# Scores of two slots in one visit of TensorE, with the last 64 keys in spare PSUM columns

## The chip, the cores and the metric

The kernel runs on one NeuronCore of a Trainium2 chip. The metric is device time in microseconds (us) of one execution. TensorE (PE) does matrix products into PSUM, an accumulator memory of eight banks with 512 fp32 columns on each of 128 partitions. VectorE (DVE), ScalarE (ACT) and GpSimd (POOL) do elementwise work; POOL does not touch PSUM. SyncE (SP) issues the DMA transfers of the kernel's steady part. Each engine works through its own list of instructions in order, and engines wait for each other through semaphores.

## The reference, cut to what matters

Attention with a top-k mask over 8 batches, 8 heads, 576 queries and keys and head size 64, followed by a two-layer block with a quick GELU on the 4608 x 512 result:

```python
scores = scale * np.matmul(q, k.transpose(0, 1, 3, 2))          # 576 x 576 per head
kth = np.partition(scores, -32, axis=-1)[..., -32:-31]
scores = np.where(scores >= kth, scores, -1e9)
attn = exp(scores - max); attn = attn / (sum(attn) + 1e-9)
x = (attn @ v) rearranged to (4608, 512)
h = x @ w_in                                                      # 512 -> 2048
out = (h / (1 + np.exp(-1.702 * h))) @ w_out                      # 2048 -> 512
```

## The kernel before, in words

The attention is cut into 144 **slots**. A slot is 128 rows of queries of two heads (64 rows of four heads for a head's last 64 queries, the "ends"); 18 slots make a batch. Odd batches begin with their two ends slots (heads 0 to 3, then heads 4 to 7), even batches end with them. For each slot the kernel does, in this order:

- `scores(n)` on PE: 8 products of 64 x 64 weights with 288 keys. They contract over 64 rows, so PE's array is split into four quadrants that work side by side. All four banks of the one tile `s_ps` are written: bank (head, half), 288 columns of each.
- `copy_scores(n)` on ACT: both heads' 576 scores to SBUF (tile `sc`), two instructions. `pair_up(n)` on DVE: maximum and minimum of the first half (from PSUM) against the second (from `sc`); after it and the copy, `s_ps` is free for the next slot.
- `find(n, 8)` on DVE: the 32 largest of each row by MAX8 and MATCH_REPLACE8. Inside it stand `pair_up(n+1)` (after 8 of its 14 instructions) and the reciprocal of slot n-1's sums (`invert`, after the next).
- `bounds(n)` on POOL: the row's threshold and maximum (`cut`, `low`). `mask(n)` and `exps(n)` on ACT (together `exponentials`): mask and exponential with row sums `den`.
- `invert(n)`: POOL adds 1e-9 (`some`), DVE takes the reciprocal (`rden`). `normalize(n)` on POOL. `split(n)`: ACT copies the words apart (2304 16-bit values per row), SP writes them to DRAM (`rows`). `turn_by_dma(n)`: SP issues a transposing DMA to `pt`.
- `values_of_two` on PE: the products with v for two slots, into two banks `o` of the pool `ps_t`. It begins with the last 64 keys (four quadrants again, tile `v_e`), then come the 512 others with all 128 rows of the array (`v_l`). `x_of_two` on ACT copies the result to `xT`.

The two-layer block fills PE in between: `hidden` (x @ w_in, 64 matmul instructions into a `ps_t` bank called `ph`), `tanh(True)` (ACT: tanh to `th`, then a copy `h` that frees the bank), `gate` and `combine` (POOL), and `project_one` (56 matmul instructions into `po`). An fp32 product is two matmul instructions. The pool `ps_t` has two banks, used in turn: hidden, hidden, o, o in each pair.

From slot 21 on, slots go in **pairs** (`steady_pair(n)`, n odd); the order on each engine is as written in that function, without a scheduler:

- PE: project, hidden, hidden around `scores(n+2)` (one `hidden` on either side of it), project, `scores(n+3)`, values of slots n-3 and n-2.
- ACT: exponentials(n-1); every second pair the previous result leaves `po` (`leave_parts`, L770); `prepare_some` (L268, `halves`: the queries and keys of a coming batch, one pair of heads at a time); split(n-1); copy_scores(n+2); mask(n), exps(n); two `tanh(True)`; split(n); copy_scores(n+3); x_of_two.
- POOL: normalize(n-1), gate, bounds(n), combine, normalize(n), gate, bounds(n+1), combine.
- SP: rows of n-1, what is due (`write_all`, `begin(0)`), the transpose for n-1, rows of n, `turns`, `begin(1)`, the transpose for n.

The queries and keys of a coming batch are transposed by DMA too (L282, `qk_t`). For odd batches b > 1 the last two pairs of heads are transposed at slot 18b-3 (`TURN = -3`, in `begin(0)` of pair n = 18b-3), since their buffers are taken until then; the second ends slot 18b+1 is the first that needs them.

Of the kernel before, what the change touches and what calls it, by code (L numbers as in the profile page):

```python
# [11 lines left out]
F32 = mybir.dt.float32  # L12
# [7 lines left out]
P = 128  # L20
# [13 lines left out]
def kernel(  # L34
# [27 lines left out]
    nc = tc.nc  # L62

    B, H, S, D = q.shape
# [3 lines left out]
    NF = S // P  # L68
    FULL = NF * P
    TAIL = S - FULL  # L70
    HALF = S // 2
# [7 lines left out]
    FIRST = (TAIL, 0)  # L79
# [9 lines left out]
    PAIRED = SETTLED + 1  # L89
    STEADY = PAIRED + 2  # L90
    WHOLE = 2
    RING = 7
    assert D == 64 and 2 * TAIL == P and C == NP * P and C == PIECE and B % 2 == 0
    assert TOPK == 32 and NP == 4 and NF == 4 and NG == 4 and CC == 4
# [2 lines left out]
    pool = lambda name, bufs, **kw: ctx.enter_context(tc.tile_pool(name=name, bufs=bufs, **kw))  # L97
    raws = const.tile([P, RING, 2 * PIECE], U32, name="raws")
    loads = pool("loads", 1)
    v_main = const.tile([P, NP, 2, NF, D], F32, name="v_l")  # L100
    qkt = pool("qkt", 6)
    scp = pool("scp", 4)
# [6 lines left out]
    diagonals = const.tile([P, 2, P], F32, name="by")  # L109
# [3 lines left out]
    score_banks = pool("ps_s", 1, space=PSUM).tile([P, 2, 2, 512], F32, name="s_ps")  # L113
    ps_t = pool("ps_t", 2, space=PSUM)
# [12 lines left out]
    def load_piece(n):  # L127
# [3 lines left out]
        else:  # L131
            src = moe_w_in[c * P : (c + 1) * P, g * PIECE : (g + 1) * PIECE]
        raw[n] = raws[:, n % RING, :]
        nc.sync.dma_start(raw[n], src.bitcast(U32))
# [29 lines left out]
    qT, kT, vv = {}, {}, {}  # L164
# [128 lines left out]
    def write_all():  # L293
        while writes:
            writes.pop(0)()
# [9 lines left out]
    slots = []  # L305
# [7 lines left out]
    st = [{} for _ in slots]  # L313

    def head_at(n, i):

        return 1 - i if n % 2 and slots[n][0] > 0 else i

    def scores(n):
        b, t, hps = slots[n]  # L320
        ps = score_banks
        quadrants = (0, 0), (1, 1), (0, 1), (1, 0)
        of = lambda p: slice(t * P + p * TAIL, t * P + (p + 1) * TAIL) if t < NF else slice(FULL, S)
        parts = [(i, p, slice(p * TAIL, (p + 1) * TAIL), of(p)) for i, p in quadrants]
        for c in range(2):
            for i, p, rows, cols in parts:
                on = slice(head_at(n, i) * D, (head_at(n, i) + 1) * D)
                nc.tensor.matmul(  # L328
                    ps[rows, i, c, 0:HALF],
                    lhsT=qT[b, hps[p]][on, cols],  # L330
                    rhs=kT[b, hps[p]][on, FIRST[i] + c * HALF : FIRST[i] + (c + 1) * HALF],
                )

    def copy_scores(n):
        ps = score_banks
        sc = st[n]["sc"] = scp.tile([P, 2, S], F32, name="sc")
        for i in range(2):
            to = sc[:, i, :].rearrange("p (c k) -> p c k", c=2)
            nc.scalar.copy(out=to, in_=ps[:, i, :, 0:HALF])  # L339
# [3 lines left out]
    def pair_up(n):  # L343

        b = st[n]["sc"][:, :, HALF:S]
        a = score_banks[:, :, 0, 0:HALF]
        ranked[n] = rank.tile([P, 2, 2, HALF], F32, name="ranked")
        for c, op in enumerate((ALU.max, ALU.min)):
            nc.vector.tensor_tensor(out=ranked[n][:, :, c, :], in0=a, in1=b, op=op)  # L349
# [47 lines left out]
    def exponentials(n, between=lambda: None):  # L397

        mask(n)
        between()  # L400
        exps(n)
# [220 lines left out]
    class Block:  # L622
        def __init__(self, place, rows):
            self.place, self.rows = place, rows
            self.whole = len(blocks_seen) < WHOLE
            blocks_seen.append(self)
# [91 lines left out]
    def weight_sums(to, x, y):  # L718

        def part(i, j):  # L720
            of = lambda name: half(name, i)[:, 2 * j : 2 * j + 2, :, :]
            nc.gpsimd.tensor_tensor(out=of(to), in0=of(x), in1=of(y), op=ALU.subtract)

        return [lambda i=i, j=j: part(i, j) for i in range(2) for j in range(2)]
# [7 lines left out]
    def project(put_off_leaving=False):  # L732
# [56 lines left out]
        if x.done == FC:  # L789
            leaving.append(leave if x.whole else leave_parts)  # L790
            if x is blocks_seen[WHOLE - 1]:
                summing.extend(weight_sums("t3", "b22", "b12"))
# [5 lines left out]
    def merge_some(count, engine=nc.gpsimd):  # L798
        for _ in range(min(count, len(merging))):
            merging.pop(0)(engine)  # L800
# [3 lines left out]
    def leave_all():  # L804
        while leaving:
            leaving.pop(0)()
# [17 lines left out]
    for n in by_slot:  # L824
        first = sum(map(len, list(by_slot.values())[:n]))
# [102 lines left out]
    def slot(n):  # L928
# [71 lines left out]
        if n == SETTLED:  # L1000
            copy_scores(n + 2)
# [16 lines left out]
    def dues(n):  # L1018

        preparing = prepare_by_dma, prepare_by_pe  # L1020
        todo = [later.pop(m, []) for m in (n, n + 1)]
        assert not any(fn in preparing for fn, _ in todo[1])

        def begin(i):
            for fn, args in todo[i]:
                if fn not in preparing:
                    fn(*args)

        some = [(fn, args) for fn, args in todo[0] if fn in preparing]

        def prepare_some():
            if some:
                fn, args = some.pop(0)
                fn(*args)

        return begin, prepare_some

    live = lambda m: 0 <= m < N
# [12 lines left out]
    def project_one():  # L1051
        if may_project(0):
            project(True)
# [95 lines left out]
    def steady_pair(n):  # L1149

        begin, prepare_some = dues(n)
        if live(n - 1):
            exponentials(n - 1)
        combine()
        merge_some(3)
        if n > STEADY + 8:
            project_one()
        hidden(ps_t)
        if n == STEADY + 8:
            tanh(True)  # L1160
            hidden(ps_t)
        leave_all()
        prepare_some()
        find(n, 8)
        if live(n + 2):
            scores(n + 2)
        hidden(ps_t)
        if live(n - 1):
            normalize(n - 1)
            split(n - 1)  # L1170
        write_all()
        gate()
        begin(0)
        if live(n - 1):
            turn_by_dma(n - 1)
        if live(n + 2):
            copy_scores(n + 2)
        if live(n):
            bounds(n)
        combine()  # L1180
        merge_some(3)
        if live(n):
            mask(n)
            exps(n)
        tanh(True)
        tanh(True)
        prepare_some()
        project_one()
        find(n + 1, 8)
        if live(n + 3):  # L1190
            scores(n + 3)
        held = [m for m in (n - 3, n - 2) if live(m)]
        o = [ps_t.tile([P, 512], F32, name="o", tag="tp")[:, 0:P] for _ in held]
        values_of_two(held, o)
        if live(n):
            normalize(n)
            split(n)
        write_all()
        while turns:
            turns.pop(0)()  # L1200
        begin(1)
        if live(n):
            turn_by_dma(n)
        gate()
        if live(n + 3):
            copy_scores(n + 3)
        x_of_two(held, o)
        if live(n + 1):
            bounds(n + 1)
# [54 lines left out]
```

## Time and profile before

| What | Value |
|---|---|
| median of 3 runs (lowest to highest) | 1384.13 us (1384.01 to 1385.76) |
| the profiled execution | 1387.0 us, of which the span of instructions 1385.2 us |
| busy share of the span | PE 97%, DVE 93%, ACT 84%, POOL 70% |
| mean granted PE clock | 0.987 |
| a steady pair (start of one `scores(n+3)` to the next) | 17.63 us in most pairs |

How to read it: times are microseconds from the start of the span. A row of the timeline has the start, the time from the first start to the last end of the instructions merged in it, engine, line, operation, output and input, shape, and count. Ends of matmuls are modelled and overlap the next group, so lengths on PE are taken from start to start. PEld is PE's weight load, which overlaps its matmuls. SPq rows are issues on SP.

### The profile page before, as it was taken

The page shows a single profiled execution, that of the slowest core. Times are in us where ns is not written, and L with a number is a line of the kernel's source. Part 1 is how long each engine was busy: PE and PEld are TensorE (multiplying, and loading weights), DVE is VectorE, ACT ScalarE, POOL GpSimd, SP SyncE. Part 2 cuts the span into 40 slices and gives each one's busy share as a digit, 9 for nine tenths or more (in the row PEclk, how much of TensorE's full clock was granted, in tenths as well). Part 3 has the DMA queues.
Part 4 walks back from the last instruction along what each step waited for, and adds up shares of the span by engine and source line. Part 5 has one row for each costly group of instructions (what it writes and reads, how often), then busy time and mean ns, then how long its engine had stood idle before and what let it go on. Part 6 is the DMA issues. An engine that isn't in the chain of part 4 may idle for free. (4 is left out here: it accounts for less than half of the span.)

```text
span 1385.2 us, 54404 instructions
## 1 busy us (share of the span) xinstructions
PE 1345.7 (97%) x22560; PEld 1209.1 (87%) x22560; DVE 1283.0 (93%) x3392; ACT 1165.2 (84%) x1930; POOL 963.8 (70%) x1758
## 2 busy tenths in 40 slices
PE   7889889999999999999999999999999999999998
PEld 5676568899998999999999999999999999999997
DVE  7999889999999999999999999999999999999912
ACT  6888778999998998999998998889998998888831
POOL 3777586677777777777776777777777777777770
PEclk9899999999999999999999999999999999999999
DMA  8552556988889776977798678887898878855640
GB/s 231 161 151 67 128 150 160 212 200 199 199 208 206 177 184 174 237 198 196 194 203 223 181 187 193 193 195 200 197 213 208 196 182 182 183 139 138 155 111 17
DMA packets 527223, 246.92 MB, mean 178 GB/s; under 512 B 458880, under 2 KB 505472, under 8 KB 526976
## 3 DMA queue, kind: packets, MB, share of 16 engines
q1 hardware_dynamic: 526544, 243.16, 71.7%
q8 instruction: 177, 2.90, 0.9%
q14 instruction: 70, 0.57, 0.1%
q10 hardware_dynamic: 432, 0.30, 0.1%
HBM read 46.01 MB, written 103.42 MB: 108 GB/s over the span
## 5 line engine op out<-in xcount | busy, mean ns | idle before, releaser
L375 DVE MAX8 top<-ranked 128x8 f32<-128x288 f32 (+1 forms) x1152 | 637.4, 595 | 0.0
L646 PEld LDWEIGHTS ph<-xT,win 128*64 128x64 f32 (+1 forms) x8736 | 479.7, 137 | 28.9 <-issue 25.0
L646 PE MATMUL ph<-xT,win 128*64 128x128 f32 (+1 forms) x8736 | 504.5, 273 | 0.0
L379 DVE MATCH_REPLACE8 ranked<-top,ranked 128x288 f32<-128x288 f32 (+1 forms) x864 | 462.3, 542 | 0.0
L479 ACT COPY sc<-pr 128x2304 uint16<-128x2304 uint16 x134 | 283.4, 2115 | 100.9 <-POOL pr L443 100.9
L443 POOL TENSOR_SCALAR pr<-pr,rden 128x576 f32<-128x576 f32 x268 | 198.0, 750 | 53.6 <-DVE rden L430 53.0
L417 ACT ACTIVATE pr<-sc,low 128x576 f32<-128x576 f32 x288 | 220.1, 771 | 0.0
L407 ACT ACTIVATE sc<-sc,cut 128x576 f32<-128x576 f32 x288 | 208.9, 781 | 5.6 <-POOL cut L393 5.6
L752 PE MATMUL po<-raws,h 128*64 128x128 f32 x2112 | 205.1, 273 | 0.2 <-POOL h L700 0.2
L752 PE MATMUL po<-wout,h 128*64 128x128 f32 x2112 | 205.2, 273 | 0.1
L349 DVE TENSOR_TENSOR ranked<-s_ps,sc 128x576 f32<-128x576 f32 x286 | 201.8, 747 | 0.3 <-ACT sc L339 0.3
L339 ACT COPY sc<-s_ps 128x576 f32<-128x576 f32 x286 | 168.5, 642 | 21.0 <-PE s_ps L328 13.6
L328 PE MATMUL s_ps<-qk_t 64*64 64x288 f32 x2304 | 177.5, 422 | 8.1 <-DVE ranked L349 7.7
L426 POOL TENSOR_SCALAR some<-den 128x2 f32<-128x2 f32 x132 | 29.3, 222 | 222.0 <-ACT pr L417 221.7
L675 POOL TENSOR_TENSOR th<-th,h 128x512 f32<-128x512 f32 x134 | 171.8, 1282 | 11.2
L752 PE MATMUL po<-wout,th 128*64 128x128 f32 x2176 | 165.2, 273 | 0.0
L752 PEld LDWEIGHTS po<-wout,h 128*64 128x64 f32 x2112 | 133.4, 137 | 0.6 <-POOL h L701 0.6
L752 PEld LDWEIGHTS po<-raws,h 128*64 128x64 f32 x2112 | 133.4, 137 | 0.5 <-POOL h L700 0.5
L328 PEld LDWEIGHTS s_ps<-qk_t 64*64 64x64 f32 x2304 | 76.1, 134 | 61.6 <-issue 14.4
L752 PEld LDWEIGHTS po<-wout,th 128*64 128x64 f32 x2176 | 127.7, 137 | 0.9 <-POOL low L394 0.4
L575 PE MATMUL o<-pt,v_l 128*64 128x128 f32 (+1 forms) x2240 | 124.8, 265 | 0.0
L575 PEld LDWEIGHTS o<-pt,v_l 128*64 128x64 f32 x2240 | 110.3, 137 | 10.1 <-issue 9.6
(111 smaller groups left out, 1631.3 us busy)
## 6 DMA issues: line engine op xcount, KB each, us to landing
rows<-sc SPq DMA_DIRECT2D x134, 576.0 KB, 3.8
qk_rows<-halves SPq DMA_DIRECT2D x24, 576.0 KB, 5.6
out_dram<-raws SPq DMA_DIRECT2D x68, 128.0 KB, 3.6
raws<-in_moe_w_in_dram SPq DMA_DIRECT2D x16, 512.0 KB, 4.9
raws<-in_moe_w_out_dram SPq DMA_DIRECT2D x16, 512.0 KB, 3.6
qk_l<-in_q_dram SPq DMA_DIRECT2D x28, 256.0 KB, 4.4
qk_l<-in_k_dram SPq DMA_DIRECT2D x28, 256.0 KB, 4.3
v_l<-in_v_dram SPq DMA_DIRECT2D x4, 1024.0 KB, 7.8
```

The lines of the kernel that those rows point to most:

```text
L328: nc.tensor.matmul(ps[rows, i, c, 0:HALF], lhsT=qT[b, hps[p]][on, cols], rhs=kT[b, hps[p]][on, FIRST[i] + c * HALF : FIRST[i] + (c + 1) * ...
L349: nc.vector.tensor_tensor(out=ranked[n][:, :, c, :], in0=a, in1=b, op=op)
L375: nc.vector.max(top[:, i, 8 * r : 8 * r + 8], of(r, i))
L379: nc.vector.match_replace(to, top[:, i, 8 * r : 8 * r + 8], of(r, i), LOWEST)
L407: nc.scalar.activation(sc[:, i, :], sc[:, i, :], AF.Prelu, bias=cut[:, i : i + 1], scale=SCALE, alpha=HUGE)
L417: nc.scalar.activation(pr[:, i * S : (i + 1) * S], sc[:, i, :], AF.Exp, bias=low[:, i : i + 1], accum_out=den[:, i : i + 1],)
L443: nc.gpsimd.tensor_scalar(pr[:, i, :], pr[:, i, :], st[n]["rden"][:, i : i + 1], 1.0, op0=ALU.mult, op1=ALU.mult)
L479: nc.scalar.copy(out=halves, in_=pr[:].bitcast(U16).rearrange("p (k h) -> p h k", h=2))
L575: nc.tensor.matmul(o[s][j * D : (j + 1) * D, cols], lhsT=lhsT, rhs=rhs, start=(s, j) not in halves[:k], stop=(s, j) not in halves[k + 1 :],)
L646: nc.tensor.matmul(ph[rows, i * P : (i + 1) * P], lhsT=win[:, c, f * P + rows.start : f * P + rows.stop], rhs=xs[:, x.place, c, :], start= ...
L675: nc.gpsimd.tensor_tensor(out=th[:], in0=th[:], in1=h, op=ALU.mult)
L752: nc.tensor.matmul(both_banks[y * TAIL : (y + 1) * TAIL, bank, to * P : (to + 1) * P], lhsT=a[:, i, :], rhs=weight(w, fs[i])[:, y, :], sta ...
```

## The change

`TOGETHER` is 24. From slot 24 on, scores are no longer taken slot by slot. In the second half of pair n, `scores_of_two` computes slots n+3 and n+4 one after the other, directly ahead of `values_of_two`. Of a head's 576 keys, 512 go to one whole bank of `s_ps` (slot parity and head choose the bank, so two slots fit in the four banks), and 64 go to columns 128 to 255 of the two `o` banks, whose first 128 columns the values use. Per slot the PE instructions are 8 of 512 and 8 of 64 columns, where they were 16 of 288.

`copy_asides` brings the 64-column parts to SBUF with four ACT copies per pair (64 partitions x 128 elements) into `by` (the tile `diagonals`). `copy_new` fills `sc` per slot: POOL copies the 64 keys of both heads out of `by`, ACT copies 1024 elements in one instruction. For slot n+4 that happens in the next pair, where `copy_scores` of that slot stood before; for slot n+3 at the end of this pair, between `gate` and `x_of_two`. `pair_up` reads the first 288 columns of the new banks. DVE's and SP's lists stay as they were. In the built program the first read of an `o` bank by `copy_asides` waits for the last matmul into that bank, which is one of the values'; the first write of the 64 columns into an `o` bank waits for the ACT copy `h` of the `ph` that had the bank.

```diff
+    TOGETHER = STEADY + 11
...
+    def scores_of_two(ms, aside):
+        for s, m in enumerate(ms):
+            b, t, hps = slots[m]
+            quadrants = (0, 0), (1, 1), (0, 1), (1, 0)
+            for first, count in ((0, FULL), (FULL, TAIL)):
+                for i, p in quadrants:
+                    rows = slice(p * TAIL, (p + 1) * TAIL)
+                    cols = slice(t * P + p * TAIL, t * P + (p + 1) * TAIL) if t < NF else slice(FULL, S)
+                    on = slice(head_at(m, i) * D, (head_at(m, i) + 1) * D)
+                    to = score_banks[rows, m % 2, i, :] if first == 0 else aside[head_at(m, i) ^ p][rows, P + s * TAIL : P + (s + 1) * TAIL]
+                    nc.tensor.matmul(
+                        to,
+                        lhsT=qT[b, hps[p]][on, cols],
+                        rhs=kT[b, hps[p]][on, FIRST[i] + first : FIRST[i] + first + count],
+                    )
+
+    kept = diagonals[:].rearrange("p a (c k) -> p (a c) k", c=2)
+
+    def copy_asides(aside):
+        blocks = slice(0, 4, 3), slice(1, 3)
+        for p in range(2):
+            rows = slice(p * TAIL, (p + 1) * TAIL)
+            for bank in range(2):
+                both = aside[bank][rows, P : 2 * P].rearrange("p (s k) -> p s k", s=2)
+                nc.scalar.copy(out=kept[rows, blocks[bank ^ p], :], in_=both)
+
+    def copy_new(m, s):
+        sc = st[m]["sc"] = scp.tile([P, 2, S], F32, name="sc")
+        nc.gpsimd.tensor_copy(out=sc[:, :, FULL:S], in_=kept[:, 2 * s : 2 * s + 2, :])
+        nc.scalar.copy(out=sc[:, :, 0:FULL], in_=score_banks[:, m % 2, :, :])
...
     def pair_up(n):
         b = st[n]["sc"][:, :, HALF:S]
-        a = score_banks[:, :, 0, 0:HALF]
+        a = score_banks[:, :, 0, 0:HALF] if n < TOGETHER else score_banks[:, n % 2, :, 0:HALF]
...
     def steady_pair(n):
         find(n, 8)
-        if live(n + 2):
+        if n + 2 < TOGETHER:
             scores(n + 2)
...
-        if live(n + 2):
+        if n + 2 < TOGETHER:
             copy_scores(n + 2)
+        elif live(n + 2):
+            copy_new(n + 2, 1)
...
         find(n + 1, 8)
-        if live(n + 3):
-            scores(n + 3)
         held = [m for m in (n - 3, n - 2) if live(m)]
-        o = [ps_t.tile([P, 512], F32, name="o", tag="tp")[:, 0:P] for _ in held]
+        banks = [ps_t.tile([P, 512], F32, name="o", tag="tp") for _ in held]
+        o = [bank[:, 0:P] for bank in banks]
+        ahead = [m for m in (n + 3, n + 4) if live(m)]
+        scores_of_two(ahead, banks)
         values_of_two(held, o)
...
         gate()
-        if live(n + 3):
-            copy_scores(n + 3)
+        if ahead:
+            copy_asides(banks)
+            copy_new(n + 3, 0)
         x_of_two(held, o)
```

## The prediction

> **What bounds the kernel now.** I read the page's first part, then the busy times of the steady stretch, then one pair on each engine, the chain from DVE and POOL into ACT, and last SP's queue. The page and the stretch first (columns: us, then busy us of PE, weight load, DVE, ACT, POOL, then clock):
>
> ```profile
> PE 1345.7 (97%) x22560; PEld 1209.1 (87%) x22560; DVE 1283.0 (93%) x3392; ACT 1165.2 (84%) x1930; POOL 963.8 (70%) x1758
> ...
> 701.36:718.99 17.63, 17.63 (x314) 16.14 (x313) 17.47 (x47) 15.15 (x25) 14.20 (x28) 1.00 0.85 186
> ```
>
> PE is never idle in this pair, at full clock, and DVE nearly so. Whether PE really streams is seen from start to start:
>
> ```profile
> 267.19 1.20 PE L328 MATMUL s_ps<-qk_t 64*64 64x288 f32 x16
> ...
> 701.36 1.20 PE L328 MATMUL s_ps<-qk_t 64*64 64x288 f32 x16
> 702.49 3.71 PE L646 MATMUL ph<-xT,win 128*64 128x128 f32 x64
> 706.04 0.61 PE L752 MATMUL po<-wout,th 128*64 128x128 f32 x8
> ...
> 709.19 1.20 PE L328 MATMUL s_ps<-qk_t 64*64 64x288 f32 x16
> 710.22 0.40 PE L575 MATMUL o<-pt,v_e 64*64 64x128 f32 x8
> 710.54 1.97 PE L575 MATMUL o<-pt,v_l 128*64 128x128 f32 x32
> 712.34 0.61 PE L752 MATMUL po<-wout,th 128*64 128x128 f32 x8
> ...
> 715.40 3.66 PE L646 MATMUL ph<-xT,win 128*64 128x128 f32 x64
> 718.99 1.20 PE L328 MATMUL s_ps<-qk_t 64*64 64x288 f32 x16
> ...
> 1292.37 1.20 PE L328 MATMUL s_ps<-qk_t 64*64 64x288 f32 x16
> ```
>
> The pair takes 718.99 - 701.36 = 17.63 us, and every group runs at its rate: a project (56 instructions, two at a time on two halves of the columns) 715.40 - 712.34 = 3.06, so 0.109 per 128 columns; 64 of hidden 3.55. From pair 23 to pair 139 it is (1292.37 - 267.19) / 58 = 17.68 per pair, 17.63 with few exceptions. So PE's list bounds the kernel, and anything else that stays under 17.63 is free.
>
> **PE's own work.** The first scores last 702.49 - 701.36 = 1.13, the second 710.22 - 709.19 = 1.03. The second has a four-quadrant group behind it, the first returns to 128 rows: 0.10 dearer. The project ahead of scores takes 709.19 - 706.04 = 3.15 where 3.06 is its rate: 0.09 for going in. hidden behind scores takes 3.55 against 32 x 0.109 = 3.49, some 0.05 more, and I give scores' first round the same 0.05. One visit to the quadrants so costs 0.10 + 0.05 in and 0.10 + 0.05 out: 0.30. The change removes one visit per pair: -0.30.
>
> Four instructions, one per quadrant, run as a round. A round of 288 columns is (1.03 - 0.05) / 4 = 0.245; with 0.109 for 128 that is 0.85 ns per column. So 512 columns are 0.435 (estimate), 64 columns 0.055 by that slope, or no cheaper than 0.109 if a weight load cannot hide under so short a round; the trace has no shorter one than 0.109. Per pair: before 8 x 0.245 = 1.96, after 4 x 0.435 + 4 x (0.055 to 0.109) = 1.96 to 2.18. PE's list alone would go to 17.63 - 0.30 + (0 to 0.22) = 17.33 to 17.55.
>
> Here a rule of the Trainium skill speaks against the change. The page TensorEngine Tiling (Array Packing), section Restrictions and Gotchas, says: "Different row tiles cannot access same PSUM bank simultaneously". The 64-column products of both row halves write to the same `o` bank. The trace does not agree: the row at 710.22 does that already for the values (both row halves of a slot into one bank), and its two rounds with the way out take 0.32 = 2 x 0.109 + 0.10. By the row the sharing costs nothing; by the rule the four 64-column rounds of a pair would take twice their time, 0.22 to 0.44 more.
>
> **ACT's chain, where I see the new bound.** The rows of ACT, DVE and POOL from one end of the values (712.34, call it T) on:
>
> ```profile
> 711.05 1.17 ACT L339 COPY sc<-s_ps 128x576 f32<-128x576 f32 x2
> 712.11 0.28 ACT L589 COPY xT<-o 128x128 f32<-128x128 f32 x1
> 712.57 0.27 ACT L589 COPY xT<-o 128x128 f32<-128x128 f32 x1 [0.18 <-PE o L575]
> 712.73 1.44 ACT L407 ACTIVATE sc<-sc,cut 128x576 f32<-128x576 f32 x2
> ...
> 715.50 0.19 ACT L417 ACTIVATION_READ_ACCUMULATOR pr<-sc,low 128x1 f32 x1
> 717.80 2.11 ACT L479 COPY sc<-pr 128x2304 uint16<-128x2304 uint16 x1 [2.12 <-POOL pr L443]
> 720.26 1.18 ACT L339 COPY sc<-s_ps 128x576 f32<-128x576 f32 x2 [0.34 <-PE s_ps L328]
> 721.33 1.45 ACT L407 ACTIVATE sc<-sc,cut 128x576 f32<-128x576 f32 x2
> ...
> 725.62 0.61 ACT L665 COPY h<-ph 128x512 f32<-128x512 f32 x1
> ...
> 730.78 0.45 ACT L589 COPY xT<-o 128x128 f32<-128x128 f32 x2
> ```
>
> ```profile
> POOL some L426 <- ACT pr L417: 221.7, 129, 3.4
> ...
> 715.77 0.22 POOL L426 TENSOR_SCALAR some<-den 128x2 f32<-128x2 f32 x1 [1.32 <-ACT pr L417]
> 716.03 0.17 DVE L430 RECIPROCAL rden<-some 128x2 f32<-128x2 f32 x1
> 716.29 1.47 POOL L443 TENSOR_SCALAR pr<-pr,rden 128x576 f32<-128x576 f32 x2 [0.30 <-DVE rden L430]
> ...
> 719.72 0.23 POOL L393 TENSOR_SCALAR cut<-top 128x4 f32<-128x4 f32 x1
> ```
>
> This is one chain: T, `xT` at T + 0.23, mask and exps of n-1 from T + 0.39 to 715.69, POOL's `some`, DVE's reciprocal (716.03 to 716.20), normalize, split at 717.80, copies, mask and exps of n, two tanh with their `h`, the last of which ends at 726.23 = T + 13.89. The wait list shows that its links really wait (129 times, 221.7 us, harmless so far). PE needs that `h` only where the values open the second `o` bank, at T + 17.63 - (712.34 - 710.22) = T + 15.51. Slack: 1.6.
>
> The change lengthens the chain and moves up its end. Copies first: one of 128 elements adds 0.45 - 0.28 = 0.17 when it follows another, one of 576 (712.11 - 711.05) / 2 = 0.53, so 1024 elements 0.53 + 448 x 0.8 ns = 0.89.
>
> - After T the second aside copy starts at T + 0.23, as `xT` did; three of the four come after T (0.51), then copy_new (0.89), then both `xT` (0.34). Mask starts at T + 1.97 instead of T + 0.39. Before, the copies of n+3 were done ahead of T.
> - From mask to split 717.80 - 712.73 = 5.07; a split 2.00 (from start to start of such a copy, below); copy_new 0.89; from mask to the end of the last `h` 726.23 - 721.33 = 4.90. Sum: 1.97 + 5.07 + 2.00 + 0.89 + 4.90 = T + 14.83.
> - PE's first 64-column round writes both `o` banks, so it waits for that `h`: about T + 14.93 with a tenth for the semaphore. PE's list reaches this place at 3.06 + 2 x 3.49 + 3.15 + 0.05 + 2 x 0.435 = T + 14.1. It now waits 0.8 us per pair.
> - From there: 0.11 to 0.22 for this slot's 64-column rounds, 0.87 and 0.11 to 0.22 for the next slot, 0.32 and 1.80 for the values: T' = T + 18.14 to 18.36. I take 18.25, the middle.
>
> Against 17.63 that is +0.62 in each of 59 pairs between two such visits (pairs 21 to 139): **+36.6 us**.
>
> What lies beside it: POOL's copy of 128 elements (between 0.23, the `cut` row, and 0.74, half of the normalize row; by columns 0.34) stands ahead of `cut`, which would come at T + 5.53 + (719.72 - 716.29) + 0.34 = T + 9.3, done by T + 9.53; mask(n) starts at T + 9.93. Cover 0.4, else its excess joins the chain. DVE needs 8.63 per find (731.31 - 722.68, below), 17.3 per pair, and gets a wait of some 1 us at the reciprocal; harmless under 18.25. The `xT` copies end at T + 2.1, hidden needs them at T + 3.06. `pair_up(n+2)`, for which both slots' products wait, ends at T + 1.97 + (716.03 - 712.73) + (722.68 + 1.42 - 716.03) = T + 13.34; two 512-column rounds later it is T + 14.3, 0.6 ahead of the `h`.
>
> **Where ACT has more in the chain.** In every second pair a result leaves and a copy for the next batch stands between exps and split:
>
> ```profile
> 722.68 1.42 DVE L349 TENSOR_TENSOR ranked<-s_ps,sc 128x576 f32<-128x576 f32 x2
> 731.31 1.42 DVE L349 TENSOR_TENSOR ranked<-s_ps,sc 128x576 f32<-128x576 f32 x2
> ...
> 733.96 0.98 ACT L770 ACTIVATE raws<-po 128x512 f32<-128x512 f32 x2
> 734.81 2.14 ACT L268 COPY halves<-qk_l 128x2304 uint16<-128x2304 uint16 x1
> 736.81 2.15 ACT L479 COPY sc<-pr 128x2304 uint16<-128x2304 uint16 x1
> ...
> L268 ACT COPY halves<-qk_l x24: 2112/2115/2146, 240.3 to 1123.1; 128x2304 uint16<-128x2304 uint16 x24
> ```
>
> 736.81 - 733.96 = 2.85, in a gap of 717.80 - 715.69 = 2.11: 0.74 too long. Leaves and copies both come every four slots, so the 23 copies after 248 us each have one: 23 x 0.74 = **+17.0**; 0 if they part company.
>
> **What is late next: three batches' keys.** Slot 18b+1 of odd b was scored in pair 18b-1 and now in pair 18b-3, the one that issues its transposes:
>
> ```profile
> 512.50 6.77 SPq L282 DMA_TRANSPOSE qk_t<-qk_rows  x2
> ...
> L282 SPq DMA_TRANSPOSE qk_t<-qk_rows x24: 2626/3846/5239, 256.7 to 1151.2; - x24
> ...
> DMA to landing us min/median/max: 6.3/6.9/8.3
> ...
> 514.67 1.20 PE L328 MATMUL s_ps<-qk_t 64*64 64x288 f32 x16
> ...
> 524.47 1.20 PE L328 MATMUL s_ps<-qk_t 64*64 64x288 f32 x16
> ```
>
> This is b = 3, whose pair has its T at 514.67 + (712.34 - 709.19) - 17.63 = 500.2. SP issues at T + 12.3, the second of the two 2.6 (the shortest issue) to 3.4 (half) later; I take T + 15.0, and it lands 6.9 after that: T + 21.9. Before, 524.47 was in time by 2.4. Now PE gets there at T + 15.1 and waits 6.8; with the shortest landing 6.2, with the longest 8.2. I take 6.5 for each of b = 3, 5 and 7: **+19.5**. SP's list is unchanged, so nothing moves these issues up; even batches transpose theirs a pair earlier.
>
> **Sum.** 1387.0 (the profiled execution) + 36.6 + 17.0 + 19.5 - 2.6 (the odd long pairs of before, 58 x 0.045, that the new wait swallows) = 1457.5. That execution is 2.9 above the median of 1384.1, so 1454.6 against the median, +5.1%. The bounds of the 64-column rounds move it by 6 each way, the 23 pairs down by 17, the keys by -1 to +5, the semaphore and copy estimates by 0.1 per pair, 6. The likeliest case's own range is 1425 to 1475.
>
> **Rivals.**
>
> - *ACT's chain fits* (it ends before T + 14.1: 0.8 us of my sum is wrong). For it: ACT is busy only 15.15 of 17.63, and 4 x 0.17 + 2 x 0.89 - 4 x 0.53 = 0.34 more work goes into it. Against: its idle time is those 2.1 us of waiting for POOL and DVE, in the chain. Then PE gains 59 x (0.08 to 0.30) = 5 to 18. With the keys' wait of 19.5 that is 1386 to 1399: chance 0.09.
> - *Faster*: PE remains the bound, as its busy row of 97% says, and stays so in the three batches. Place: the pair's first 64-column round; the point: nothing that PE waits for there or behind comes after T + 14.1. 1384 less 5 to 18: 1366 to 1379, chance 0.04. Against: the keys' landing alone.
> - *The keys cost nothing*, because the chain's own delay covers them: 1454.6 - 19.5 = 1435, chance 0.11. Against: 21.9 is well over 18.25.
> - *A second wait* in the chain: POOL's copy, `cut` and the merges of a leaving result delay mask(n) or `some(n)` by half a us or more per pair: +30 or more, 1485 to 1515. For it: cover of only 0.4. Chance 0.07.
> - *The banks take turns.* If row halves did so, each 64-column round would take twice its time: 59 x (0.22 to 0.44) = 13 to 26 more, about 1475. Against: the row at 710.22. Chance 0.03. The Trainium skill's page TensorEngine Tiling (Array Packing), section Restrictions and Gotchas, has this as a rule.
>
> **How the numbers follow.** My case has 0.66. Leaving out the second wait (0.07) above and the first two rivals (0.13) below, the range is 1415 to 1485. 0.2% of the time, 2.8 us, is about what a measurement of this kernel tells from no change. Faster comes from the second rival, same from the edge of the first: 0.04, 0.02, slower 0.94.
>
> **What would show it.** Steady pairs of some 18.2 us, 19 where both L770's and L268's successors stand; PE idle ahead of the 64-column rounds with ACT's `h` named; 0.5 us more of ACT between the values' end and mask for the asides; DVE waiting about 1 us at the reciprocal; PE waiting 6 us for `qk_t` near slots 55, 91 and 127. It would be wrong if PE's pairs stayed under 17.63, if mask started before T + 1.5, or if PE's wait named DVE or POOL.

## The result and the profile after

The changed kernel takes 1463.89 us (median of 6 runs, 1463.36 to 1465.74), the kernel before in the same session 1384.95 (1383.45 to 1389.93): ratio 1.0567, 95% interval 1.0549 to 1.0584. The profiled execution has a span of 1461.8 us against 1385.2. Line numbers below are those of the kernel that the row is from; in the changed kernel L346 is scores, L361 the aside copies, L367 the 1024-column copy, L442 the mask, L452 exps, L514 split, L610 values, L700 `h`, L787 project.

The page's busy line and its chain that ended last (PE had 47% of that chain before):

```profile
PE 1364.0 (93%) x22560; PEld 1214.5 (83%) x22560; DVE 1285.6 (88%) x3392; ACT 1193.3 (82%) x2050; POOL 990.5 (68%) x1878
...
ACT 26%; DVE 22%; PE 13%; issue 9%; POOL 8%; DMA 2%; SPq 1%; ACTq 0%; POOLq 0%; DVEq 0%
```

No engine is full any more. A plain pair, the next one with a leaving result and `halves` in it, and a stretch behind a late key transpose (columns as in the prediction):

```profile
705.61:723.97 18.36, 17.72 (x317) 16.25 (x315) 16.82 (x44) 14.95 (x26) 13.03 (x26) 1.00 0.88 211
...
723.97:742.98 19.01, 17.95 (x317) 16.13 (x314) 18.02 (x51) 17.81 (x29) 13.52 (x27) 1.00 0.71 195
...
528.00:541.00 13.00, 10.61 (x120) 8.18 (x122) 5.77 (x17) 5.31 (x10) 3.81 (x9) 0.74 0.54 134
```

Pairs alternate between 18.36 and 19.01. Taken from the start of one pair's values to the next, the pairs of slots 51, 87 and 123 take 23.61, 24.69 and 24.19, and the pairs behind them 20.42, 19.02 and 20.14; uneven pairs of the experiments below are taken in the same way, unless they are said to go from T to T. T is the end of the values, as in the prediction. ACT in the pair that starts at T = 705.61:

```profile
705.84 0.69 ACT L361 COPY by<-o 64x128 f32<-64x128 f32 x3 [0.62 <-PE o L610]
706.55 1.01 ACT L367 COPY sc<-s_ps 128x1024 f32<-128x1024 f32 x1
707.46 0.44 ACT L624 COPY xT<-o 128x128 f32<-128x128 f32 x2
707.78 1.46 ACT L442 ACTIVATE sc<-sc,cut 128x576 f32<-128x576 f32 x2
...
712.86 2.11 ACT L514 COPY sc<-pr 128x2304 uint16<-128x2304 uint16 x1 [2.11 <-POOL pr L478]
714.87 1.01 ACT L367 COPY sc<-s_ps 128x1024 f32<-128x1024 f32 x1
715.78 1.44 ACT L442 ACTIVATE sc<-sc,cut 128x576 f32<-128x576 f32 x2
...
720.07 0.59 ACT L700 COPY h<-ph 128x512 f32<-128x512 f32 x1
721.48 2.11 ACT L514 COPY sc<-pr 128x2304 uint16<-128x2304 uint16 x1 [0.82 <-POOL pr L478]
```

The mask starts at T + 2.17, the last `h` ends at 720.66 = T + 15.05. PE in the same pair:

```profile
705.61 0.61 PE L787 MATMUL po<-wout,th 128*64 128x128 f32 x8
...
719.25 1.09 PE L346 MATMUL s_ps<-qk_t 64*64 64x512 f32 x8 [0.37 <-ACT th L697]
720.13 0.31 PE L346 MATMUL o<-qk_t 64*64 64x64 f32 x4
720.71 0.27 PE L346 MATMUL o<-qk_t 64*64 64x64 f32 x2 [0.27 <-ACT h L700]
720.74 0.65 PE L346 MATMUL s_ps<-qk_t 64*64 64x512 f32 x2
...
721.65 0.31 PE L346 MATMUL o<-qk_t 64*64 64x64 f32 x6
721.77 0.28 PE L610 MATMUL o<-pt,v_e 64*64 64x128 f32 x2
...
723.97 0.61 PE L787 MATMUL po<-wout,th 128*64 128x128 f32 x8
```

PE waits twice. The first wait ends with `pair_up` of the other slot, whose last row on DVE ends at 719.15; the profile names `th`, which ends almost with it. The second time PE waits for the `h` that ends at 720.66. It goes on at T + 15.10, and the next pair starts 3.26 later. The list of waits (us in total, times, longest) has that `h` 120 times; before, a wait of values for `h` stood there with 1.5 us, 2 times:

```profile
POOL sc L366 <- ACT by L361: 131.6, 60, 9.2
...
DVE rden L465 <- POOL some L461: 80.3, 69, 3.7
...
PEld o L346 <- ACT h L700: 62.8, 120, 1.2
ACT by L361 <- PE o L610: 62.2, 88, 6.8
```

The late keys of batch 3, on SP and on PE:

```profile
523.48 5.90 SPq L283 DMA_TRANSPOSE qk_t<-qk_rows  x2
```

```profile
529.12 1.07 PE L346 MATMUL s_ps<-qk_t 64*64 64x512 f32 x2 [1.84 <-DMA qk_t<-qk_rows]
531.46 1.13 PE L346 MATMUL s_ps<-qk_t 64*64 64x512 f32 x3 [1.27 <-DMA qk_t<-qk_rows]
```

With PE's idle time at the keys comes a stretch of half clock: between 528 and 541 the granted clock is 0.74, which is 6.8 us at half speed in 13, and the same 0.74 stands in the 13 us from 869 and from 1214. So part of the six long pairs is clock, not waiting.

### The profile page after: what moved, and what is told of

Read it like the earlier page. It is cut to its first block, busy times and chain, and to the rows that moved or that the text cites. A ratio compares the mean times of both kernels' runs of the same rounds, so it can differ in the third digit from the quotient of the medians.

```text
span 1461.8 us, 54728 instructions
## 1 busy us (share of the span) xinstructions
PE 1364.0 (93%) x22560; PEld 1214.5 (83%) x22560; DVE 1285.6 (88%) x3392; ACT 1193.3 (82%) x2050; POOL 990.5 (68%) x1878
## 4 chain that ended last, share of the span: by engine, by line
ACT 26%; DVE 22%; PE 13%; issue 9%; POOL 8%; DMA 2%; SPq 1%; ACTq 0%; POOLq 0%; DVEq 0%
DVE top L410 11%; DVE ranked L414 8%; ACT pr L452 7%; PE o L610 6%; ACT sc L367 4%; ACT sc L514 3%; ACT sc L442 3%; ACT h L700 2%; PE po L787 2%; PE s_ps L346 2%; DVE ranked L384 2%; PE ph L681 2%; ACT halves L269 2%; POOL raws L809 2%; POOL pr L478 1%
## 5 line engine op out<-in xcount | busy, mean ns | idle before, releaser
L681 PE MATMUL ph<-xT,win 128*64 128x128 f32 (+1 forms) x8736 | 491.3, 273 | 0.0
L514 ACT COPY sc<-pr 128x2304 uint16<-128x2304 uint16 x134 | 283.7, 2117 | 120.9 <-POOL pr L478 120.9
L452 ACT ACTIVATE pr<-sc,low 128x576 f32<-128x576 f32 x288 | 220.3, 773 | 0.0
L442 ACT ACTIVATE sc<-sc,cut 128x576 f32<-128x576 f32 x288 | 209.4, 784 | 5.6 <-POOL cut L428 5.5
L787 PE MATMUL po<-raws,h 128*64 128x128 f32 x2112 | 205.1, 273 | 0.8 <-POOL h L735 0.8
L787 PE MATMUL po<-wout,h 128*64 128x128 f32 x2112 | 205.1, 273 | 0.1
L346 PE MATMUL s_ps<-qk_t 64*64 64x512 f32 x960 | 141.6, 617 | 34.8 <-ACT th L697 14.6
L787 PE MATMUL po<-wout,th 128*64 128x128 f32 x2176 | 165.2, 273 | 0.0
L346 PEld LDWEIGHTS o<-qk_t 64*64 64x64 f32 x960 | 56.3, 134 | 99.0 <-ACT h L700 62.8
L787 PEld LDWEIGHTS po<-raws,h 128*64 128x64 f32 x2112 | 133.4, 137 | 1.0 <-POOL h L735 1.0
L787 PEld LDWEIGHTS po<-wout,h 128*64 128x64 f32 x2112 | 133.3, 137 | 0.6 <-POOL h L736 0.6
L787 PEld LDWEIGHTS po<-wout,th 128*64 128x64 f32 x2176 | 127.9, 137 | 1.0 <-POOL th L710 0.6
L610 PE MATMUL o<-pt,v_l 128*64 128x128 f32 (+1 forms) x2240 | 128.2, 270 | 0.0
L366 POOL COPY sc<-by 128x128 f32<-128x128 f32 x120 | 34.9, 291 | 131.6 <-ACT by L361 131.6
L367 ACT COPY sc<-s_ps 128x1024 f32<-128x1024 f32 x120 | 121.9, 1016 | 1.5
L610 PEld LDWEIGHTS o<-pt,v_l 128*64 128x64 f32 x2240 | 113.6, 140 | 10.6 <-issue 9.6
```

Source lines behind the costliest of these rows:

```text
L346: nc.tensor.matmul(to, lhsT=qT[b, hps[p]][on, cols], rhs=kT[b, hps[p]][on, FIRST[i] + first : FIRST[i] + first + count],)
L367: nc.scalar.copy(out=sc[:, :, 0:FULL], in_=score_banks[:, m % 2, :, :])
L442: nc.scalar.activation(sc[:, i, :], sc[:, i, :], AF.Prelu, bias=cut[:, i : i + 1], scale=SCALE, alpha=HUGE)
L452: nc.scalar.activation(pr[:, i * S : (i + 1) * S], sc[:, i, :], AF.Exp, bias=low[:, i : i + 1], accum_out=den[:, i : i + 1],)
L514: nc.scalar.copy(out=halves, in_=pr[:].bitcast(U16).rearrange("p (k h) -> p h k", h=2))
L610: nc.tensor.matmul(o[s][j * D : (j + 1) * D, cols], lhsT=lhsT, rhs=rhs, start=(s, j) not in halves[:k], stop=(s, j) not in halves[k + 1 :],)
```

## The experiments

**Two rows of pairs that the theory explains one by one.** First the keys alone:

```diff
-        if b % 2 and hp > 1:
-            at(b * PER + TURN, turn)
+        if b % 2 and hp == 2:
+            at(b * PER + TURN - 1, turn)
         else:
             turns.append(turn)
```

> The changed kernel with the transposes of an odd batch's last two pairs of heads issued about half a pair sooner: in the second half of pair 18b-5, right behind the scores that free their buffers. Nothing else differs. Theory (three batches' keys come too late): the long pairs 51, 53, 87, 89, 123 and 125 (5.2, 2.1, 6.3, 0.7, 5.8 and 1.8 us over their neighbours, 21.9 in all) go, 1464 becomes 1442; the other pairs stay at 18.36 and 19.01. Rival (those long pairs come from the load on the DMA queues at a batch's start, whatever the order): 1464, or a stall that only moves to another pair, within 5 us of 1464.

Measured: 1444.92 us, ratio 1.0421 (1.0405 to 1.0436), 20 us less by the difference of the ratios. The six long pairs are gone (18.37 each), and with them the stretches of half clock. All other pairs stay at 18.37 and 19.02: the keys are a cost of their own.

Then the copy into `halves`, parted between POOL and ACT:

```diff
-        nc.scalar.copy(out=halves[:], in_=words.rearrange("p c (e h) -> p c h e", h=2))
+        parts = words.rearrange("p c (e h) -> p c h e", h=2)
+        nc.gpsimd.tensor_copy(out=halves[:, 0:4, :, :], in_=parts[:, 0:4, :, :])
+        nc.scalar.copy(out=halves[:, 4:, :, :], in_=parts[:, 4:, :, :])
```

> The changed kernel with the copy into halves (2.1 us, ScalarE, every second pair) parted: four of its nine blocks go to GpSimd, five stay, so that a leaving result (0.85) and the rest (1.2) fit the 2.1 us for which ScalarE waits for GpSimd. Theory: pairs of 19.01 become 18.36 to 18.5, 23 x 0.5 to 0.65 = 12 to 15 us less: 1449 to 1452. The rival (GpSimd, which makes the sums that ScalarE waits for, is late by as much as it takes over, 1.5 to 2 us) says 19.01 stays or grows: 1464 to 1485.

Measured: 1449.32, ratio 1.0453 (1.0436 to 1.0469). All pairs of 19.01 are at 18.37: this term, too, is what it was taken for.

The same two edits in the kernel before:

> The kernel before with two of the edits that made the changed kernel faster by 19 and 15 us: odd batches' last two key transposes a pair earlier, and the copy into halves parted between GpSimd and ScalarE. Theory (before is bound by TensorE's own list, keys are in time there, and the longer chain of a leaving result and halves still fits): no change, 1386 +- 4, ratio 0.998 to 1.002. The rival (these edits help any kernel, so they say nothing of the change) says 10 to 35 us less: 1351 to 1376.

Measured: 1384.92, ratio 1.0004 (0.9995 to 1.0013). Nothing. What these edits gain in the changed kernel, the change had put in.

**Is it the 0.4 us at the first 512-column round?** In the changed kernel both slots' scores are one tile, so PE's first round waits for the readers of the other slot as well. Two tiles in place of one:

```diff
-    score_banks = pool("ps_s", 1, space=PSUM).tile([P, 2, 2, 512], F32, name="s_ps")
+    ps_s = pool("ps_s", 1, space=PSUM)
+    score_banks = [ps_s.tile([P, 2, 512], F32, name=name) for name in ("s_ps", "s_pt")]
```

> The changed kernel with the score banks of odd and even slots as two PSUM tiles in place of one, so that the products of a slot wait only for the readers of its own bank; nothing else. The theory (the next pair's values are held by ScalarE's chain, which ends in the copy of h) says that the 0.5 us for which the first 512-column round waits for pair_up only moves to the 64-column round, which waits for h: pairs stay at 18.36 and 19.01, 1464 +- 4 us. The rival (the wait for pair_up, which comes from the two slots sharing a tile, is part of what sets the pair) says 0.3 to 0.5 us less per pair: 1434 to 1446.

Measured: 1464.82, ratio 1.0565 (1.0548 to 1.0581). PE in a plain pair:

```profile
721.21 1.09 PE L346 MATMUL s_ps<-qk_t 64*64 64x512 f32 x8
...
723.11 0.33 PE L346 MATMUL o<-qk_t 64*64 64x64 f32 x4 [0.64 <-ACT h L698]
```

The first wait has gone, and the second is longer by as much (0.64 = 0.37 + 0.27); pairs are 18.36 and 19.01 as before. So it is the wait for `h` that sets the pair.

**Lengthening the chain.** The 1024-column copy of slot n+3, done twice:

```diff
             copy_new(n + 3, 0)
+            nc.scalar.copy(out=st[n + 3]["sc"][:, :, 0:FULL], in_=score_banks[:, (n + 3) % 2, :, :])
```

> The changed kernel with the 1024-element copy of slot n+3 done twice in a row on ACT, 0.91 us more per pair; the second writes the same values again. Theory (chain): all of it shows, 59 x 0.91 = 54 us more, about 1518, pairs of 19.27 and 19.92. Rival (ACT has idle time to spare, PE or DMA set the pace): 1464 to 1470.

Measured: 1550.73, ratio 1.1185 (1.1159 to 1.1211), by the difference of the ratios 86 us more than the changed kernel. Where the clock is full, pairs are 19.41 and 20.07, 1.05 longer than in the changed kernel; the second copy starts 1.05 after the first. So each us of ACT in this place is a us of the pair: 59 x 1.05 = 62, where 54 were expected. In other stretches the pairs are 19.95 and 21.02, and there the granted clock drops again and again:

```profile
404.00:416.00 12.00, 10.09 (x146) 7.65 (x144) 12.00 (x36) 9.50 (x14) 8.14 (x16) 0.86 0.43 127
```

0.86 over 12 us is a stretch of 3.4 us at half speed; in these parts of the run such stretches come every 40.96 us. Ahead of this one PE had stood still twice:

```profile
409.11 1.09 PE L346 MATMUL s_ps<-qk_t 64*64 64x512 f32 x8 [1.25 <-DVE ranked L384]
...
411.19 0.37 PE L346 MATMUL o<-qk_t 64*64 64x64 f32 x2 [0.64 <-ACT h L700]
```

From T to T the pairs with such a stretch are 21.6, 1.5 us longer than 20.07, and there are 15 of them: the lost clock is the other part of the 86. But the same two waits do not always bring the clock down. From 640 to 836 they stand in every second pair, at full clock:

```profile
658.41 1.09 PE L346 MATMUL s_ps<-qk_t 64*64 64x512 f32 x8 [1.24 <-DVE ranked L384]
...
660.50 0.27 PE L346 MATMUL o<-qk_t 64*64 64x64 f32 x2 [0.64 <-ACT h L700]
...
640.00:836.00 196.00, 179.48 (x3116) 161.32 (x3110) 173.21 (x458) 172.67 (x283) 132.69 (x265) 1.00 0.76 181
```

**Was there slack in the kernel before?** The prediction gave its chain 1.6 us to spare. The two copies of slot n+3 there, done twice:

```diff
             copy_scores(n + 3)
+            for again in range(1):
+                for i in range(2):
+                    to = st[n + 3]["sc"][:, i, :].rearrange("p (c k) -> p c k", c=2)
+                    nc.scalar.copy(out=to, in_=score_banks[:, i, :, 0:HALF])
```

> The kernel before with the two copies of slot n+3 done twice on ACT, 1.06 us more per pair; the second pass writes the same values again. Theory (the same chain had 1.6 us to spare in the kernel before, mask starts only about 0.7 later): no change, pairs stay at 17.63, 1385 within 4 us. Rival (any work added to ACT at this place lengthens the pair): 60 x 0.7 to 1.06 = 42 to 64 us more, 1427 to 1449.

Measured: 1421.42, ratio 1.0250 (1.0234 to 1.0266). The theory falls in this point: pairs are 17.94 and 18.64 in turn, and the kernel is 35 us longer. ACT between one split(n) and the next, and PE's wait:

```profile
705.99 2.11 ACT L479 COPY sc<-pr 128x2304 uint16<-128x2304 uint16 x1 [0.65 <-POOL pr L443]
708.01 1.18 ACT L339 COPY sc<-s_ps 128x576 f32<-128x576 f32 x2
709.07 1.20 ACT L1210 COPY sc<-s_ps 128x576 f32<-128x576 f32 x2
...
710.45 1.49 ACT L407 ACTIVATE sc<-sc,cut 128x576 f32<-128x576 f32 x2
```

```profile
PEld o L575 <- ACT h L665: 37.6, 62, 0.8
```

There is a second loop, which does not go through PE at all: ACT's own list, with the waits for POOL and DVE that stand in it. Split ends, the copies and both `xT` follow without a gap, mask and exps, POOL and DVE make `pr`, split, and so on to the next split(n); in this run ACT waits for PE nowhere in it. Its length here is the pair, 17.94 and 18.64, so without the 1.06 us of repeated copies it would be 16.88 and 17.58, in the mean 17.23 against PE's 17.63. By this subtraction, an estimate, the kernel before had 0.4 us per pair to spare, not 1.6: the 1.6 were counted along the way from the values, and the other way round the loop was not looked at.

**Shortening the chain.** The 1024-column copy of slot n+3, done between the scores of n+3 and n+4, so that ACT does it while it waits for POOL ahead of split(n). The first two lines stand in `scores_of_two`, behind the products of a slot; in the old place only POOL's 128 columns are left:

```diff
+            if s == 0:
+                copy_main(m)
...
-            copy_new(n + 3, 0)
+            copy_last(n + 3, 0)
```

> The changed kernel with one ACT instruction moved: the 1024-element copy of slot n+3 stands behind the two tanh, ahead of split(n), where ACT idles 0.82 us, and no longer between the values' end and the next mask. Same work on every engine. Theory (the chain through ACT sets the pair): mask starts 0.91 sooner, the pair goes from 18.36 to about 17.45 and from 19.01 to 18.10, 59 x 0.91 = 54 us less, about 1410; if PE's own list (17.33 to 17.55) takes over, 1410 to 1416. Rival (PE's own groups have become dearer, by the short rounds or by sharing banks): 1464, as PE's work is the same.

Measured: 1510.40, ratio 1.0889 (1.0850 to 1.0927), slower instead of faster. The list of waits has a new line:

```profile
PE s_ps L346 <- ACT sc L368: 51.3, 57, 3.0
```

With one tile for both slots, the products of slot n+4 now wait for the copy of slot n+3: PE stands 0.9 us in the mean. The run decides nothing between the theory and the rival, since the edit put in a wait. The same edit with the two tiles of the run above:

> The same two tiles, and the 1024-element copy of slot n+3 issued between the products of slot n+3 and slot n+4, ahead of the split of slot n, so that it fills a wait of ScalarE for GpSimd and no longer stands between the values' end and the mask. Two loops are left: through TensorE, 18.36 less a copy of 0.9 = 17.45, and ScalarE's own list, 17.9 less one copy of 0.8 to 0.9 = 17.1 (0.7 more in pairs with a leaving result and halves). TensorE's own list is 17.33 to 17.55. So the theory says pairs of 17.45 to 17.6, with the extra work 18.1, the three late-key pairs as before: 1464 - 59 x 0.85 = 1414, 1405 to 1425. The rival (the pair is long because the 64-column rounds and the 512-column rounds cost TensorE more, and the wait for h is only where that shows) says that the pair stays at 18.2 to 18.4: about 1460. If the new place makes another wait, as in the run without the two tiles, the trace names ScalarE's copy ahead of the products of slot n+4.

Measured: 1447.95, ratio 1.0452 (1.0423 to 1.0482). Pairs are 17.98 and 18.33, where they were 18.36 and 19.01: the place was right, but the gain is 0.38 in the plain pairs and 0.68 in the others, not 0.9. The early copy also waits 14 times, 17.5 us in all, for its buffer, whose older contents are still being written out, and the pairs with such a wait take up to 21. What became of the other 0.5 us shows in the run with all four edits (two tiles, early copy, keys, parted `halves`):

> All of it: two score tiles, the early copy, the two key transposes of odd batches a pair earlier, and the parted copy into halves. By the theory every pair is at 17.45 to 17.6, which is TensorE's own list (17.33 to 17.55): against the kernel before (17.63 and 17.68 in the mean) 59 x 0.05 to 0.25 less, 1370 to 1383, so a little faster than the kernel before. If the parted copy fails, 23 x 0.6 more: 1384 to 1397. If the rival on TensorE's rounds were right, 1425 to 1440.

Measured: 1418.29, ratio 1.0224 (1.0205 to 1.0244), some 35 us above the expected range; pairs are 18.00 and 17.88. PE, ACT and POOL behind a T of 668.48:

```profile
668.48 0.61 PE L797 MATMUL po<-wout,th 128*64 128x128 f32 x8
...
668.70 0.70 ACT L365 COPY by<-o 64x128 f32<-64x128 f32 x3 [0.44 <-PE o L620]
669.42 0.43 ACT L634 COPY xT<-o 128x128 f32<-128x128 f32 x2
669.99 1.44 ACT L452 ACTIVATE sc<-sc,cut 128x576 f32<-128x576 f32 x2
...
669.46 0.29 POOL L374 COPY sc<-by 128x128 f32<-128x128 f32 x1 [1.55 <-ACT by L365]
669.73 0.23 POOL L438 TENSOR_SCALAR cut<-top 128x4 f32<-128x4 f32 x1
```

The mask starts at T + 1.51, right behind `cut` (669.73 + 0.23 = 669.96). POOL's 128-column copy waits 1.55 us for the aside copies, and `cut`, which needs nothing of them, stands behind it. So the two operations of `bounds` ahead of that copy:

```diff
+        if live(n + 1):
+            bounds(n + 1)
         if ahead:
             copy_asides(banks)
             copy_last(n + 3, 0)
         x_of_two(held, o)
-        if live(n + 1):
-            bounds(n + 1)
```

> The run with all four edits (1418), and the two small operations of GpSimd that make cut for the next mask issued ahead of its 128-column copy instead of behind it. In that run the mask starts 1.51 us after the end of the values, 0.14 after ScalarE's last copy, because cut stands behind a GpSimd copy that waits for the aside copies. Theory: mask 0.12 to 0.14 earlier, pairs 18.00 to 17.87, 59 x 0.13 = 8 us less: 1410, 1406 to 1414. The rival (what is left of the pair, 18.0 against TensorE's 17.5, is not on the way from the values to the mask) says 1418 unchanged.

Measured: 1395.76, ratio 1.0085 (1.0066 to 1.0104), 19 us less by the difference of the ratios, where 8 were expected. Pairs are 17.45 to 17.52, which is PE's own list. The rows, T = 664.91:

```profile
666.17 1.45 ACT L452 ACTIVATE sc<-sc,cut 128x576 f32<-128x576 f32 x2
...
671.24 2.11 ACT L524 COPY sc<-pr 128x2304 uint16<-128x2304 uint16 x1
```

```profile
664.33 0.23 POOL L438 TENSOR_SCALAR cut<-top 128x4 f32<-128x4 f32 x1
...
669.22 0.22 POOL L471 TENSOR_SCALAR some<-den 128x2 f32<-128x2 f32 x1 [0.15 <-ACT pr L462]
```

The mask is 0.25 earlier (T + 1.26), and from mask to split it takes 5.07 instead of 5.26 (in the plain pairs 5.14 instead of 5.38): `cut` and `low` had also stood, with their 0.5 us, in POOL's list between the aside copy and `some`, for which the chain waits. One edit of POOL's order counted at two places.

Then the mask itself ahead of the aside copies, in the 0.44 us for which ACT waits for the values (the next pair then begins with exps alone):

```diff
         if live(n + 1):
             bounds(n + 1)
+            mask(n + 1)
         if ahead:
             copy_asides(banks)
```

> The same, and the mask of the next slot issued ahead of the aside copies, in the 0.44 us for which ScalarE waits for the values. exps then follow the copies of xT directly: they start 2.25 us after the end of the values instead of 2.86, the last h ends 0.6 to 0.7 earlier than in the run with four edits, which is more than TensorE's wait of 0.5 there. Theory: TensorE's own list, 17.33 to 17.55 (17.49 by that run's own rows less its wait), is the pair again, and only the waits of the early copy for a score buffer are left over it (14 times, 16 us, of which half may be covered): 1418 - 59 x 0.5 = 1389, 1380 to 1398. The rival (the pair stays near 18.0 whatever ScalarE's order is) says 1410 to 1418.

Measured: 1435.68, ratio 1.0373 (1.0357 to 1.0388), 40 us worse than without. Pairs are 18.36 and 18.47. ACT and POOL, T = 471.89:

```profile
474.13 0.79 ACT L462 ACTIVATE pr<-sc,low 128x576 f32<-128x576 f32 x1
...
479.25 2.11 ACT L524 COPY sc<-pr 128x2304 uint16<-128x2304 uint16 x1 [3.49 <-POOL pr L488]
```

```profile
473.85 0.29 POOL L374 COPY sc<-by 128x128 f32<-128x128 f32 x1 [2.01 <-ACT by L365]
...
476.00 1.15 POOL L819 TENSOR_TENSOR raws<-raws 128x128 f32<-128x128 f32 x2
477.23 0.22 POOL L471 TENSOR_SCALAR some<-den 128x2 f32<-128x2 f32 x1
```

exps start at T + 2.24, as expected. But the aside copies come later, POOL's copy starts at T + 1.96 (T + 0.98 above), and behind it stand four operations of `combine` and the merges; `some` comes at T + 5.34 instead of the T + 4.31 above, though exps end at 475.8 (475.57 and 0.19 of the last read). The chain changed from ACT's list to POOL's.

**What is left, and a version that is faster.** With `cut` ahead the pairs are PE's, except eleven of 18.6 to 21.9, in which the early copy waits for a score buffer. A fifth one, paid with a tanh buffer and a place for `xT`:

```diff
-    scp = pool("scp", 4)
+    scp = pool("scp", 5)
-    PLACES = 4
+    PLACES = 3
-    thp = pool("thp", 8)
+    thp = pool("thp", 7)
```

> The run with cut ahead (1396, pairs of 17.45 to 17.51 and eleven longer ones of 18.6 to 21.9), with a fifth score buffer, for which one of eight tanh buffers and one of four places for xT are given up. In that run the early copy of slot n+3 waited 19 times, 22.5 us in all, for the write of an older slot's halves out of the same buffer. Theory: these waits go, the long pairs come down to 17.5 to 18, 20 to 25 us less: 1371 to 1376, faster than the kernel before by about 0.8%; pairs are TensorE's own list. The rival (fewer tanh buffers and places make a new wait, ScalarE for the project's reads of th and h) says 17.6 or more per pair, 1380 to 1396.

Measured: 1381.08, ratio 0.9964 (0.9951 to 0.9978): faster than the kernel before, by 0.36%, about half of what was expected. All six runs are below all eleven of the kernel before in the same session (at most 1382.66 against at least 1383.09). Two pairs of it:

```profile
677.00:712.00 35.00, 35.00 (x630) 32.19 (x628) 34.73 (x92) 31.93 (x55) 27.68 (x55) 1.00 0.91 201
```

PE is full again, and the steady pairs are 17.46 and 17.53 against 17.63. What keeps the gain below 59 x 0.13 = 8 us is six longer pairs (18.0 to 18.7). In five of them PE waits for a transposed `pt`, 0.2 to 0.8 us; in the sixth it waits 0.3 for `h`.

## Why the prediction was right, and where it was not

The forecast was 1454.6 in a range of 1415 to 1485; it came to 1463.9, slower by 5.7% where 5.1% was said. The mechanism was the one forecast: ACT's chain from the end of the values to the last `h`. Of the 9.3 us that it missed, the pairs make +6.4, `halves` -2.0 and the keys +2.4; 2.9 more were taken off because the profiled execution before lay above its median, which the one after does not. By its steps:

- **PE's own work.** Right. Its list alone was put at 17.33 to 17.55 per pair; where nothing else holds it, it takes 17.45 to 17.53. A 64-column round costs what the slope said: from 721.65, where the last two begin, to 721.77, where the first products of the values begin behind them, it is 0.12, so 0.06 apiece where 0.055 to 0.109 was said.
- **ACT's chain as the new bound.** Right, and shown from both sides: one us more in it is one us more per pair, and when it is made short enough PE's list returns. Behind the copies its terms were sized to 0.02: from mask to split 5.08, the split 2.01, the 1024-column copy 0.91, and from mask to the last `h` 4.88, against 5.07, 2.00, 0.89 and 4.90.
- **The copies after T.** This term was too small. The aside copies were priced at 0.17 apiece, after copies of 128 rows; these take 64 rows each and follow at 0.24 (three of them from 705.84 to 706.55). So mask started at T + 2.17 instead of T + 1.97, `h` ended at T + 15.05 instead of T + 14.83. PE went on 0.05 behind it, not 0.10, and the rest took 3.26, near the lower end of 3.21 to 3.43. So the pair is 18.36, at the upper end of 18.14 to 18.36, where 18.25 was taken. Over 59 pairs that is 43 us for 36.6, the largest part of the miss.
- **Pairs with a leaving result and `halves`.** 0.65 instead of 0.74: 15 for 17.0 us, and gone when a part of the copy moves to POOL.
- **The keys.** The landing was put too late. In the pair of slot 51, T is 511.86 and PE goes on with the second keys at 531.46 = T + 19.6, not T + 21.9. A plain pair is there at T + 15.1, so the keys add 4.5 us and not 6.5 (at slots 87 and 123 it is 5.6 and 5.1). But half clock comes with it, which no step had, and it costs more than was saved: the six pairs together are 21.9 us over 18.36 each, where 19.5 was forecast. The sum came near by two errors of opposite sign, which is luck.
- **Slack of 1.6 in the kernel before, and what ACT's idle time is.** Wrong. Repeating two copies there cost 35 us. The step followed the chain from the end of the values to `h` and compared it with PE; it left out the loop that closes through ACT's own list. For the changed kernel the omission did no harm, because there the way through PE is the longer one.
- **`pair_up` 0.6 ahead of `h`.** Right. It ended at 719.15, T + 13.54 instead of T + 13.34, and the two 512-column rounds behind it were done 0.53 ahead of `h` (720.13 against 720.66). PE waits 0.37 for it at the first round, and two tiles showed that this costs nothing.
- **DVE's wait at the reciprocal.** About 1 us was said; in the pair shown it is 1.33 (711.09), and the list of waits has 80.3 us in all against 26.7.
- **The rivals.** *ACT's chain fits* and *faster* are refuted for this kernel; they come true only with the edits of the last runs. *The keys cost nothing* is refuted too: with the keys earlier the kernel is 20 us shorter. *A second wait in POOL's list* did not occur in the changed kernel (mask(n) starts 0.6 behind `cut`), but three of the experiments ran into it. *The banks take turns*: the Trainium skill's page TensorEngine Tiling (Array Packing), section Restrictions and Gotchas, has it as a rule; the 0.06 us above, with two row halves writing into one bank, and PE's list of 17.45 speak against it. The rule would add 0.22 to 0.44 to that list. By the measurement, which decides, row halves write one bank side by side here.

## What to carry to other kernels

When an engine is 97% busy, ask of every other engine's list two things: how long is the way from the bound's release to its next wait, and how long is the list's own loop through the other engines if the bound took no time at all. Moving work earlier on the full engine moves its consumers, too: here the copies of two slots came to stand behind the values, in the one place where each of their 64-row pieces counted in full. And an operation that waits for something new holds up all that stands behind it in its engine's list, needed or not: two small POOL operations behind such a wait cost 19 us, and an order of ACT that made POOL's copy late cost 40.

## What the runs showed of the hardware

- PE's granted clock can fall to half with waits that are short against a pair. At the late keys of slot 51, with waits of 1.84 and 1.27 us, it was at half for 6.8 us, and as long at the two other late transposes. In the kernel with the repeated copy, 15 times waits of 1.25 and 0.64 us, with 1.4 us of work between them, came with 3.4 us at half. From 640 to 836 of the same run such waits left the clock full, and what decides is not shown. Pairs with waits of 0.37 and 0.27 us show a full 1.00. A wait of PE can so cost more than its length. The Trainium skill's page TensorE: Matmul & The Clock Gate, section Why this matters for your kernels, advises against idle gaps of more than about 3 us; at slot 87, where PE waited 3.11 us, the trace agrees, and at slots 51 and 123 (no wait above 2.44) and with the repeated copy half clock came with less.
- ACT's copy of 64 partitions x 128 columns took 0.24 from start to start, one of 128 x 128 a little less (0.17): half the partitions saved nothing. These copies also write two blocks of 64 columns apart, so what makes them dearer is not shown.
- In these programs a tile in PSUM is one thing to wait for: products into two of its banks waited 0.37 us for readers of the other two, and with two tiles for the same banks that wait was gone.
